# A linear-attention mixer with an MLP on one core: `wv` loaded ahead of x2, x2 and x3 in halves, and the first jobs in another order

## The chip, the core and the metric

The kernel runs on one core of a Trainium2 chip. It has five engines with an instruction stream each: TensorE (PE, matmul; PEld is its weight load), VectorE (DVE), ScalarE (ACT), GpSimd (POOL) and SyncE (SP). DMAs are issued from SP and from ACT. The metric is device time of one execution in microseconds, the median of several. The kernel before was timed three times.

## What is computed

The input x has 2048 tokens of 448 features. It is normalised; two branches work on the result, and both are added to x:

```python
x = A_x
xn = _layernorm(x, axis=-1)
return x + _A_ref(xn, A_wqkv, A_w_phi, A_wo) + _B_ref(xn, B_w1, B_w2, B_w3, B_w4)

# A: 16 heads of 28
qkv = x @ wqkv
pq, pk = q @ w_phi, k @ w_phi                       # per head
phi_q = concat(softmax(pq), softmax(-pq)); phi_k likewise
kv = phi_k^T v;  z = sum over tokens of phi_k
o = (phi_q kv) / (phi_q z + 1e-6);  return o @ wo

# B: four channel groups of gelu(layernorm(x) @ w1) shifted by 1, -1, 2, -2 tokens
h = gelu(layernorm(x) @ w1)
x1 = x + concat(shifted quarters of h) @ w2
return x1 + gelu(layernorm(x1) @ w3) @ w4
```

(The lines under A and B are shortened; the branch B normalises xn once more, which in the kernel is the same normalised tile, with its own epsilon taken in the sums.)

## The kernel before

**Recorder.** The program is written as a sequence of operations with an engine each (`Recorder.op`, L67). `solve` (L76) works out which operation has to wait for which, and every engine plays its own operations strictly in the order in which they were recorded. So the order of the text is the order on each engine, and an operation that waits holds back all that stand behind it on its engine. All matmuls carry line 204, PE transposes 208, ScalarE activations 212, element-wise operations 216, DMAs 219 (transposing) and 222.

**Loads (L351 to L388).** x is loaded as 16 tiles of 128 tokens (x0 to x15, `load_x`); weights with 448 input rows in two halves of 256 rows that overlap by 64 (`load_half`), so that each holds two chunks of 128 rows. The order on SP's queue is x0, x2, second half of `wv`, x4, second half of `w1`, x6 and x7, x8 to x11, x12 to x15, `w_phi`, then transposing DMAs of the q and k weights (`load_wT`, the first of which waits for `wv`); on ACT's queue x1, x3, first half of `wv`, x5, first half of `w1`.

**Layer norm (L453 to L487), tile by tile.** In the lists, `("m", i)` is the statistics of tile i on VectorE (`bn_stats`, `bn_aggr`), `("r", i, n)` the inverse root for n tiles from i on GpSimd (a power of -0.5, `ln_scale`), `("a", i)` subtracting and scaling on VectorE into `xn`, `("p", i)` the same on GpSimd. Tile 1's sums are made on ScalarE instead (`ln1_sums`, L470), and `("v", 1)` is its aggregate on VectorE.

**First jobs (L945 to L969).** TensorE works on the two halves of its rows at once: LO, partitions 0 to 63, and HI, 64 to 127. The jobs that `chain` (L560) plays are
- `XT(i, b)`: eight PE transposes of normalised tile i, four in each half, into PSUM banks b and b+1, then an eviction to `xnT` on ScalarE (`xn_out`, L514); `XD(i)` does the transposition by a DMA instead;
- `ZV(i)`: V of tile i, seven matmuls of 448 columns on `wv` (four in one half, three in the other), then the eviction `EV` to `vaug`;
- `ZW(g, m)`: the first MLP matrix for four tiles, seven matmuls of 512 columns on `w1`, then a GELU (`EW`);
- `FO`: the product of the k or q weights with the feature map; `ZR`, `HF`: the remaining channels of `w1`, and the first q, k and `w2` products;
- `L(...)`: layer-norm steps; `do(f)`: anything else.

For a `zip` job (ZV, ZW, ZR) `chain` puts out the LO matmuls at once and keeps the HI matmuls in a list `upper`; they are put out between later LO matmuls, not before `lag` columns (600) after the last LO matmul of their job, since both write the same PSUM bank. `inside(n, job, inner)` puts an inner job after n LO matmuls.

`spin(n, cols)` (L491) issues n dummy matmuls on all 128 rows into bank 7, on a tile `busy` that a VectorE memset has filled: 39 of 128 columns at the start, and five of 256 after the transposes of tile 0.

**The rest** is one list played in order (L1034 to L1054): feature maps, attention sums, `w2`, the second layer norm, `w3`, `w4`, `wo` and the stores.

Of the kernel before, what the change touches and what calls it, by code (L numbers as in the profile page):

```python
# [6 lines left out]
ACT = mybir.ActivationFunctionType  # L7
# [217 lines left out]
def bass_parallel_sum__linear_kernel_hedgehog__mixer_s_mlp__prompt_kernel(  # L225
# [17 lines left out]
    with es:  # L243
# [107 lines left out]
        def load_x(i, n, eng="SP"):  # L351
            R.dma(xtok[:, i:i + n, :], x2d[128 * i:128 * (i + n), :].rearrange("(j p) d -> p j d", p=128), eng)

        def load_rows(dst, src):
            R.dma(dst[:, 0:3, :], src[0:384, :].rearrange("(c p) d -> p c d", p=128))
            R.dma(dst[0:64, 3, :], src[384:448, :])
# [5 lines left out]
        def load_half(dst, src, h, eng="SP"):  # L362
            R.dma(dst[:, 2 * h:2 * h + 2, :], src[192 * h:192 * h + 256, :].rearrange("(c p) d -> p c d", p=128), eng)
# [5 lines left out]
        load_x(2, 1)  # L369
        load_x(3, 1, "ACT")  # L370
        load_half(wv, wv_d, 1)
        load_half(wv, wv_d, 0, "ACT")
        load_x(4, 1)
        load_x(5, 1, "ACT")
        load_half(w1, B_w1, 1)
        load_half(w1, B_w1, 0, "ACT")
# [13 lines left out]
        def load_w2():  # L390
            R.dma(w2[:, 0:NH, :], B_w2[0:REST, :].rearrange("(m p) d -> p m d", p=128))
            for h in range(2):
                R.dma(w2[64 * h:64 * h + 64, NH, :], B_w2[REST:D, :])

        def load_w4():
            R.dma(w4[:, :, :], B_w4.rearrange("(c p) d -> p c d", p=128))
# [14 lines left out]
        busy = gT[:, 0, 0, 0:256]  # L411
        R.ew(dve, "memset", busy, 1.0)
# [78 lines left out]
        def spin(n, cols):  # L491
            for _ in range(n):
                R.mm(banks[7][:, 0:cols], busy[:, 0:128], busy[:, 0:cols], True, True)
# [20 lines left out]
        def xn_out(i, b, n, eng):  # L514
            for j in range(n):
                d, a = (xnT[:, :, 128 * (i + j):128 * (i + j) + 128].rearrange("p c (h e) -> p c h e", h=2),
                        xn_t(b)[:, :, 256 * j:256 * j + 256].rearrange("p h (c e) -> p c h e", c=KC))
                if eng == "ACT":
                    R.act(d, a, ACT.Copy)
                else:  # L520
                    R.ew(dve, "tensor_copy", d, a)
# [380 lines left out]
        def do(f, *args):  # L902
            return "do", lambda: f(*args), ()

        def L(*ops):
            return do(ln1, *ops)
# [4 lines left out]
        def XT(i, b, n=1, eng="ACT"):  # L911
            return "both", xn_T(i, b, n), ((xn_out, i, b, n, eng),)
# [3 lines left out]

        def ZV(i, *then):
            return "zip", z_v(i, vb[i]), then
# [4 lines left out]
        def inside(n, job, inner):  # L923
            return (*job, (n, inner))
# [15 lines left out]
        def HF(p, n):  # L940
# [4 lines left out]
        vb = {0: 7, 1: 6, 2: 0, 3: 2, 4: 4, 5: 5, 6: 1, 7: 0, 8: 4, 9: 5, 10: 0, 11: 6, 12: 3, 13: 2, 14: 0, 15: 1}  # L945
        gb = ((5, 2, 3), (7, 6, 5), (4, 1, 0), (7, 7, 4))
        spin(39, 128)
        ln1_sums(1)
        chain([
            L(("m", 0), ("m", 2), ("r", 0, 1), ("a", 0), ("m", 3), ("v", 1), ("r", 1, 2), ("a", 2), ("a", 1), ("r", 3, 1)),  # L950
            XT(0, 2, 1, "ACT"), do(spin, 5, 256), L(("a", 3), ("m", 4), ("m", 5), ("r", 4, 1), ("r", 5, 1)),
            inside(1, ZV(0, EV(0, "ACT", 1)), XT(2, 5, 1, "ACT")), XT(3, 3, 1, "ACT"), ZV(2, EV(2, "ACT", 1)),
            inside(1, ZV(3, EV(3, "ACT", 1)), XT(1, 3, 1, "ACT")), ZV(1, EV(1, "ACT", 1)), L(("a", 4), ("m", 7)),
            ZW(0, 0, EW(0, 0, 1)), L(("a", 5)), XT(5, 0, 1, "ACT"),
            L(("m", 6), ("m", 9), ("r", 7, 1), ("m", 8), ("r", 6, 1), ("r", 8, 1), ("a", 7), ("a", 6), ("m", 10)), ZW(0, 2),
            L(("m", 11), ("a", 8)), XD(8), L(("m", 12)), XT(4, 0, 1, "ACT"), L(("r", 9, 1)), ZW(0, 1, EW(0, 1, 2)), L(("a", 9)),
            ZV(4, EV(4, "ACT", 1)), XD(9), XT(7, 0, 1, "ACT"), L(("r", 10, 2), ("a", 10)), XT(6, 6, 1, "ACT"), L(("m", 13)),
            ZV(5, EV(5, "ACT", 1)), do(phi_blocks), ZV(7, EV(7, "DVE", 1)), ZW(1, 1, EW(1, 1, 1)), ZV(6, EV(6, "ACT", 1)),
            L(("p", 11), ("r", 12, 1), ("m", 15)), inside(2, ZW(1, 0, EW(1, 0, 1)), XT(10, 2, 1, "ACT")), L(("r", 13, 1)),
            ZW(1, 2, EW(1, 2, 1)), L(("p", 12), ("r", 15, 1)), inside(3, ZV(8, EV(8, "ACT", 1)), FO(1, 0, 0)), L(("m", 14)),  # L960
            XD(11), L(("r", 14, 1)), do(load_wT, 0, (1, 2, 3)), L(("a", 13)), inside(1, ZV(10, EV(10, "ACT", 1)), FO(1, 0, 1)),
            L(("a", 15)), ZR(0, 7, (rest_out, 0, 7), (rest_T, 0), (h_shift, 0)), ZV(9, EV(9, "DVE", 1)), XT(12, 3, 1, "ACT"),
            L(("p", 14)), do(load_w2), XT(13, 1, 1, "ACT"), ZV(11, EV(11, "ACT", 1)), ZW(2, 2, EW(2, 2, 1)), do(late_3),
            XT(14, 2, 2, "DVE"), ZW(2, 0, EW(2, 0, 1)), ZW(2, 1, EW(2, 1, 1)), do(load_lap, w3, B_w3), FO(1, 2, 0),
            inside(3, ZW(3, 0, EW(3, 0, 1)), FO(1, 2, 1)), ZR(1, 6, (rest_out, 1, 6)),
            inside(3, ZW(3, 2, EW(3, 2, 1)), FO(0, 0, 0)), ZV(15, EV(15, "ACT", 1)), do(kv_ones),
            inside(3, ZW(3, 1, EW(3, 1, 1)), FO(0, 0, 1)), do(rest_T, 1), inside(1, ZV(14, EV(14, "ACT", 1)), FO(0, 2, 0)),
            FO(0, 2, 1), ZV(13, EV(13, "ACT", 1)), ZV(12, EV(12, "DVE", 1)), HF(0, 0), do(kv_picks), HF(1, 0), HF(2, 0), HF(0, 1),
            do(h_shift, 1), HF(1, 1), do(load_w4), HF(2, 1)], 600, 1)  # L969
# [60 lines left out]
        def wo_in():  # L1030
            load_lap(wo, A_wo)
# [3 lines left out]
            (T, 0), (T, 1), (k0, 1), (w0, 2), (kn, 0), (k1, 1), (w1_, 2), (lo, 0), (q0, 1), (k0, 2), (kx, 0), (k1, 2), (kn, 1), (w0, 4),  # L1035
            (kx, 1), (q1, 1), (T, 2), (T, 3), (q0, 2), (lo, 1), (w1_, 4), (kn, 2), (q1, 2), (T, 4), (T, 5), (lo, 3), (k0, 3), (K, 0), (k1, 3), (kn, 3),
            (kx, 2), (lo, 2), (kx, 3), (q0, 3), (sc, 0), (K, 1), (q1, 3), (T, 6), (T, 7), (A, 1), (A, 0), (k0, 4), (G, 0), (A, 3), (w0, 6),
            (A, 2), (K, 2), (k1, 4), (G, 1), (G, 2), (K, 3), (G, 3), (q0, 4), (w1_, 6), (q1, 4), (k0, 5), (K, 4), (kn, 4),
            (w0, 8), (k1, 5), (q0, 5), (kx, 4), (K, 5), (lo, 4), (w1_, 8), (kn, 5), (q1, 5), (K, 6), (k0, 6), (w0, 10),
            (k1, 6), (kx, 5), (q0, 6), (w1_, 10), (lo, 5), (q1, 6), (k0, 7), (K, 7), (kn, 6), (k1, 7), (q0, 7), (lo, 6),  # L1040
            (K, 8), (q1, 7), (lo, 7), (w0, 12), (kn, 7), (wo_in,), (kx, 6), (a, 0), (sc, 4), (w1_, 12), (b, 0), (A, 4),
            (G, 4), (A, 6), (K, 9), (A, 5), (G, 5), (G, 6), (a, 1), (K, 10), (A, 7), (K, 11), (b, 1), (a, 2), (K, 12),
            (b, 2), (kx, 7), (a, 3), (w0, 14), (a, 4), (G, 7), (lo, 9), (b, 3), (K, 13), (b, 4), (K, 14), (K, 15), (a, 5),
            (kc,), (w1_, 14), (b, 5), (kb,), (a, 6), (b, 6), (lo, 8), (N, 0), (T, 8), (a, 7), (lo, 11), (lo, 10), (f, 1, 0), (N, 1), (T, 9),
            (b, 7), (a, 8), (sc, 8), (A, 10), (A, 8), (b, 8), (f, 2, 0), (lo, 12), (A, 9), (G, 8), (A, 11), (G, 9), (a, 9),
            (G, 10), (G, 11), (a, 10), (b, 9), (lo, 13), (N, 2), (T, 10), (f, 3, 0), (b, 10), (a, 11), (f, 4, 0), (lo, 14), (N, 3), (T, 11),
            (b, 11), (a, 12), (f, 1, 1), (S, 0), (lo, 15), (N, 4), (T, 12), (sc, 12), (b, 12), (f, 2, 1), (A, 13), (A, 15), (a, 13),
            (f, 3, 1), (S, 1), (b, 13), (f, 4, 1), (a, 14), (a, 15), (A, 14), (A, 12), (S, 2), (N, 5), (T, 13), (f, 1, 2), (G, 12),
            (G, 13), (b, 14), (f, 2, 2), (b, 15), (S, 3), (N, 6), (T, 14), (a, 16), (f, 3, 2), (b, 16), (a, 17), (f, 4, 2), (a, 18),
            (G, 14), (S, 4), (b, 17), (S, 5), (N, 7), (T, 15), (f, 1, 3), (G, 15), (N, 8), (a, 19), (f, 2, 3), (b, 18), (f, 3, 3),  # L1050
            (b, 19), (f, 4, 3), (a, 20), (N, 9), (a, 21), (b, 20), (f, 1, 4), (a, 22), (N, 10), (b, 21), (S, 6), (f, 2, 4),
            (a, 23), (f, 3, 4), (b, 22), (f, 4, 4), (b, 23), (N, 11), (a, 24), (f, 1, 5), (S, 7), (a, 25), (N, 12),
            (f, 2, 5), (b, 24), (b, 25), (N, 13), (f, 3, 5), (a, 26), (f, 4, 5), (S, 8), (a, 27), (S, 9), (N, 14), (b, 26),
            (b, 27), (S, 10), (f, 1, 6), (f, 2, 6), (S, 11), (N, 15), (f, 3, 6), (S, 12), (S, 13)])  # L1054
# [34 lines left out]
```

## Time and profile before

| | us |
|---|---|
| median of three runs (lowest, highest) | 174.25 (173.88, 174.35) |
| the profiled execution | 174.06 |
| its span, first to last instruction | 172.3 |
| DVE, ACT, POOL busy | 110.9, 82.0, 90.0 |
| first matmul on `wv` | 7.57 |
| first matmul on `w1` | 11.20 |

"Busy" of TensorE counts from the issue of a matmul to its modelled end; matmuls overlap, and two run side by side on the two row halves, so busy time alone doesn't say how much was done. Times in the profile count from the first instruction of the span. The granted TensorE clock is listed as 1.00 for all stretches, but the first 128-column dummies start 107 ns apart (39 in 4.17 us), and the five 256-column ones after 5.65 us 109 ns apart: the clock doubles at about 5.1 us.

The engines during the first 14 us, as stretches: TensorE busy 5.12 of the first 7.57 us, nearly all of it dummies; 2.87 of 3.05 us from 7.57 to 10.62; 3.33 of 3.38 us to 14.00; 16.00 of 16.00 us from there to 30. VectorE is busy for 2.95 of the 3.05 us from 7.57 to 10.62, and 3.27 of the next 3.38.

### The profile page before, as it was taken

The page shows a single profiled execution, that of the slowest core. Times are in us where ns is not written, and L with a number is a line of the kernel's source. Part 1 is how long each engine was busy: PE and PEld are TensorE (multiplying, and loading weights), DVE is VectorE, ACT ScalarE, POOL GpSimd, SP SyncE. Part 2 cuts the span into 40 slices and gives each one's busy share as a digit, 9 for nine tenths or more (in the row PEclk, how much of TensorE's full clock was granted, in tenths as well). Part 3 has the DMA queues.
Part 4 walks back from the last instruction along what each step waited for, and adds up shares of the span by engine and source line. Part 5 has one row for each costly group of instructions (what it writes and reads, how often), then busy time and mean ns, then how long its engine had stood idle before and what let it go on. Part 6 is the DMA issues. An engine that isn't in the chain of part 4 may idle for free.

```text
span 172.3 us, 5315 instructions
## 1 busy us (share of the span) xinstructions
PE 166.9 (97%) x2308; PEld 96.6 (56%) x2308; DVE 110.9 (64%) x251; ACT 82.0 (48%) x107; POOL 90.0 (52%) x121
## 2 busy tenths in 40 slices
PE   7799999999999999999999999999999999999994
PEld 7545888874555555554544554554545545555563
DVE  3799943749999989918955873525817416474621
ACT  4478876777987899646133322133133212044000
POOL 5456970004779999860574289332441522724540
PEclk9999999999999999999999999999999999999999
DMA  5995546499998955161057557554961120233331
GB/s 127 330 248 92 104 67 158 87 352 220 334 159 174 135 124 138 21 76 30 11 114 97 111 105 146 94 103 106 136 135 34 30 57 4 57 34 84 88 87 50
DMA packets 51111, 20.07 MB, mean 116 GB/s; under 512 B 42256, under 2 KB 50384, under 8 KB 51088
## 3 DMA queue, kind: packets, MB, share of 16 engines
q1 hardware_dynamic: 49968, 18.86, 56.0%
q10 hardware_dynamic: 1120, 0.87, 1.6%
q8 instruction: 18, 0.29, 0.8%
q14 instruction: 5, 0.04, 0.1%
HBM read 7.14 MB, written 1.84 MB: 52 GB/s over the span
## 4 chain that ended last, share of the span: by engine, by line
PE 92%; DMA 3%; ACT 1%; DVE 1%; issue 0%; ACTq 0%
PE banks L204 91%; DMA wv<-in_A_wqkv_dram 3%; PE banks L208 1%; ACT xnT L212 1%; DVE wpq L216 1%; ACT vaug L212 0%; ACTq L222 0%; ACT L366 0%; DVE vaug L216 0%
## 5 line engine op out<-in xcount | busy, mean ns | idle before, releaser
L212 ACT ACTIVATE phik<-banks 128x1024 bf16<-128x1024 f32 (+1 forms) x44 | 42.2, 986 | 63.6 <-PE banks L204 63.4
L204 PE MATMUL banks<-gT,w 64*128 64x512 bf16 x392 | 49.2, 376 | 0.1
L216 DVE TENSOR_TENSOR vaug<-banks,vaug 128x464 f32<-128x464 f32 (+3 forms) x65 | 32.8, 513 | 20.6 <-PE banks L204 18.9
L204 PE MATMUL banks<-w,phik 64*128 64x448 bf16 (+3 forms) x434 | 45.2, 343 | 0.0
L216 POOL TENSOR_TENSOR xnT<-vaug 128x196 bf16<-128x196 f32 (+1 forms) x32 | 18.1, 587 | 47.8 <-DVE vaug L216 47.8
L204 PE MATMUL banks<-wv,xnT 64*128 64x448 bf16 (+3 forms) x222 | 32.8, 346 | 1.4 <-DMA wv<-in_A_wqkv_dram 1.2
L204 PEld LDWEIGHTS banks<-w,phik 64*128 64x128 bf16 (+1 forms) x434 | 22.9, 94 | 19.4 <-issue 0.4
L722 POOL TENSOR_TENSOR phik<-phik,rks 128x1792 bf16<-128x1792 bf16 x8 | 25.6, 3214 | 10.7 <-DVE rks L216 10.5
L204 PEld LDWEIGHTS banks<-gT,w 64*128 64x128 bf16 x392 | 18.0, 94 | 18.7 <-PE banks L204 1.1
L204 PEld LDWEIGHTS banks<-wv,xnT 64*128 64x128 bf16 (+1 forms) x222 | 13.8, 94 | 10.0 <-ACT xnT L212 1.6
L216 POOL TENSOR_TENSOR vaug<-xn,xtok 128x448 f32<-128x448 bf16 x16 | 16.2, 1033 | 0.2 <-DVE vaug L216 0.2
L216 DVE TENSOR_REDUCE ksum<-phik 128x64 f32<-128x1792 bf16 x8 | 16.0, 1994 | 0.0
L216 POOL TENSOR_TENSOR rs<-mv,mhalf 128x1 f32<-128x1 f32 (+2 forms) x18 | 12.4, 694 | 6.6 <-DVE mv L216 6.6
L204 PE MATMUL banks<-xnT,w 64*128 64x512 bf16 x84 | 15.7, 377 | 0.0
L216 DVE RECIPROCAL vaug<-banks 128x16 f32<-128x16 f32 x16 | 4.0, 252 | 17.4 <-PE banks L204 17.4
L204 PE MATMUL banks<-wpk,xnT 64*128 64x448 bf16 x112 | 14.9, 350 | 0.1
L212 ACT ACTIVATE hi<-banks 128x896 bf16<-128x896 f32 x16 | 13.8, 931 | 1.0 <-PE banks L204 1.0
L204 PE MATMUL banks<-wpq,xnT 64*128 64x448 bf16 x112 | 14.2, 349 | 0.0
L204 PE MATMUL banks<-w,hT 64*128 64x448 bf16 x96 | 12.9, 349 | 0.0
L216 DVE TENSOR_TENSOR xn<-banks,xn 128x512 bf16<-128x512 f32 (+1 forms) x16 | 9.0, 606 | 3.0 <-PE banks L204 2.9
L216 DVE BATCH_NORM_STATS2 st<-xn 128x6 f32<-128x448 bf16 x16 | 9.4, 589 | 0.0
L216 DVE BATCH_NORM_STATS2 st<-xtok 128x6 f32<-128x448 bf16 x15 | 9.1, 606 | 0.0
(72 smaller groups left out, 165.4 us busy)
## 6 DMA issues: line engine op xcount, KB each, us to landing
w<-in_B_w_dram SPq DMA_DIRECT2D x2, 896.0 KB, 5.7
out_dram<-vaug SPq DMA_DIRECT2D x15, 112.0 KB, 2.0
w<-in_B_w_dram SPq DMA_DIRECT2D x1, 1568.0 KB, 10.0
xtok<-in_A_x_dram SPq DMA_DIRECT2D x2, 448.0 KB, 7.4
wv<-in_A_wo_dram SPq DMA_DIRECT2D x2, 224.0 KB, 2.9
xtok<-in_A_x_dram SPq DMA_DIRECT2D x3, 112.0 KB, 2.6
xtok<-in_A_x_dram ACTq DMA_DIRECT2D x3, 112.0 KB, 2.8
w<-in_B_w_dram SPq DMA_DIRECT2D x1, 336.0 KB, 4.3
```

The source lines that it names most:

```text
L204: self.op("PE", lambda e: e.matmul(out, lhsT, rhs, start=start, stop=stop, skip_group_check=True), [out], [lhsT, rhs], tile=self._tile(lhsT))
L208: self.op("PE", lambda e: e.transpose(out, in_, ident), [out], [in_, ident], tile=self._tile(in_))
L212: self.op("ACT", lambda e: e.activation(out, in_, func, **kw), [out], [in_] + aps)
L216: self.op(eng, lambda e: getattr(e, name)(out, *args, **kw), [out], aps)
L722: R.op(pool, lambda e: e.tensor_tensor(ph, ph, wide, op=ALU.mult), [ph], [ph, wide, *after])
```

## The change

The transfers get another order, and x2 and x3 go in halves of 64 tokens, one on each queue. The halves of `wv` and `w1` swap queues:

```diff
+        def load_xh(i):
+            for h, eng in enumerate(("SP", "ACT")):
+                R.dma(xtok[64 * h:64 * h + 64, i, :], x2d[128 * i + 64 * h:128 * i + 64 * h + 64, :], eng)
...
         load_x(0, 1)
         load_x(1, 1, "ACT")
-        load_x(2, 1)
-        load_x(3, 1, "ACT")
-        load_half(wv, wv_d, 1)
-        load_half(wv, wv_d, 0, "ACT")
+        load_half(wv, wv_d, 0)
+        load_half(wv, wv_d, 1, "ACT")
+        load_xh(2)
+        load_xh(3)
         load_x(4, 1)
         load_x(5, 1, "ACT")
-        load_half(w1, B_w1, 1)
-        load_half(w1, B_w1, 0, "ACT")
+        load_half(w1, B_w1, 0)
+        load_half(w1, B_w1, 1, "ACT")
```

The dummy operand is a constant that the framework sets up, no longer a tile with a memset; `spin` always takes 128 columns, and `hold` makes short dummy groups on both row halves:

```diff
-        busy = gT[:, 0, 0, 0:256]
-        R.ew(dve, "memset", busy, 1.0)
+        busy = nc.const_aps.tensor(1.0, [128, 128], BF16)
+        R.rows[busy.tensor.name] = (2, False)
...
-        def spin(n, cols):
+        def spin(n):
             for _ in range(n):
-                R.mm(banks[7][:, 0:cols], busy[:, 0:128], busy[:, 0:cols], True, True)
+                R.mm(banks[7][:, 0:128], busy, busy, True, True)
+
+        def hold(b, n):
+            return [[(banks[b + k][:, 0:128], busy[r, :], busy[r, :], True) for _ in range(n)]
+                    for k, r in enumerate((slice(0, 64), slice(64, 128)))]
...
+        def HD(b, n):
+            return "both", hold(b, n), ()
```

The first jobs are re-ordered, roots are taken tile by tile, GpSimd applies tiles 3, 7, 8, 10, 12 and 14 (before: 11, 12 and 14), and `lag` goes from 600 to 200. The head of the two lists:

```diff
-        spin(39, 128)
+        spin(30)
         ln1_sums(1)
         chain([
-            L(("m", 0), ("m", 2), ("r", 0, 1), ("a", 0), ("m", 3), ("v", 1), ("r", 1, 2), ("a", 2), ("a", 1), ("r", 3, 1)),
-            XT(0, 2, 1, "ACT"), do(spin, 5, 256), L(("a", 3), ("m", 4), ("m", 5), ("r", 4, 1), ("r", 5, 1)),
-            inside(1, ZV(0, EV(0, "ACT", 1)), XT(2, 5, 1, "ACT")), XT(3, 3, 1, "ACT"), ZV(2, EV(2, "ACT", 1)),
-            inside(1, ZV(3, EV(3, "ACT", 1)), XT(1, 3, 1, "ACT")), ZV(1, EV(1, "ACT", 1)), L(("a", 4), ("m", 7)),
-            ZW(0, 0, EW(0, 0, 1)), L(("a", 5)), XT(5, 0, 1, "ACT"),
+            L(("m", 0), ("r", 0, 1), ("a", 0), ("v", 1), ("m", 2)), HD(3, 3),
+            L(("r", 1, 1), ("m", 3), ("r", 2, 1), ("r", 3, 1)), do(spin, 3), L(("a", 2)), do(spin, 3), XT(0, 2, 1, "ACT"),
+            L(("a", 1), ("m", 4)), HD(6, 3), L(("m", 5)), HD(4, 3), L(("m", 7), ("p", 3)), HD(6, 3), L(("r", 4, 1)),
+            ZV(0, EV(0, "ACT", 1)), L(("a", 4)), XT(2, 1, 1, "ACT"), do(spin, 3), L(("m", 6), ("r", 5, 1)),
+            XT(1, 5, 1, "ACT"), inside(2, ZV(2, EV(2, "ACT", 1)), XT(3, 1, 1, "ACT")), L(("m", 8)), ZV(1, EV(1, "ACT", 1)),
+            L(("r", 7, 1), ("p", 7), ("r", 6, 1), ("r", 8, 1), ("m", 11), ("a", 5), ("p", 8)), ZV(3, EV(3, "ACT", 1)),
+            XT(4, 1, 1, "ACT"), ZW(0, 0, EW(0, 0, 1)), L(("a", 6)), ZV(4, EV(4, "ACT", 1)), L(("m", 9)), XT(7, 0, 1, "ACT"),
...
-            do(h_shift, 1), HF(1, 1), do(load_w4), HF(2, 1)], 600, 1)
+            HF(0, 1), do(h_shift, 1), HF(1, 1), do(load_w4), HF(2, 1)], 200, 1)
```

The loads of `w2`, `w3`, `w4` and `wo` get a parameter for the queue, which stays SP, and `w3` is loaded by two calls in place of one that issues the same two DMAs. The long list of the rest is wrapped differently and holds the same entries in the same order. A few PSUM banks of V and of the first MLP matrix are numbered differently.

## The prediction

> **What bounds the kernel now.** The first view is the page's busy line: TensorE is at work for 97% of the span, no other engine above 64%.
>
> ```profile
> PE 166.9 (97%) x2308; PEld 96.6 (56%) x2308; DVE 110.9 (64%) x251; ACT 82.0 (48%) x107; POOL 90.0 (52%) x121
> ```
>
> The second is the chain of waits in order of time (start, length, what). From 10.62 us on it is TensorE almost without a break; before that it is the landing of `wv`, and then the evictions of transposed tiles.
>
> ```profile
> 1.74 5.70 DMA wv<-in_A_wqkv_dram
> 7.43 0.14 issue
> 7.57 0.21 PE banks L204
> ...
> 9.54 0.54 ACT vaug L212
> 10.08 0.50 ACT xnT L212
> 10.58 0.05 issue
> 10.62 1.56 PE banks L204 x12
> ...
> 86.56 83.30 PE banks L204 x1012
> ```
>
> So everything after about 10.6 us is a queue of matmuls that moves as a block. The change leaves their number and the whole written order after the first jobs as they are; its worth is how much useful TensorE work is done by the time TensorE stops starving. The third view is the DMA issues, asked for the stretches in which they were issued (KB, then us to landing): x2 and x3 (issued at 1.25), `wv` (1.71 and 1.74), x4 and x5 (2.18 and 2.22).
>
> ```profile
> xtok<-in_A_x_dram SPq DMA_DIRECT2D x1, 112.0 KB, 2.6
> xtok<-in_A_x_dram ACTq DMA_DIRECT2D x1, 112.0 KB, 2.8
> wv<-in_A_wqkv_dram SPq DMA_DIRECT2D x1, 224.0 KB, 4.8
> wv<-in_A_wqkv_dram ACTq DMA_DIRECT2D x1, 224.0 KB, 5.7
> xtok<-in_A_x_dram SPq DMA_DIRECT2D x1, 112.0 KB, 5.4
> xtok<-in_A_x_dram ACTq DMA_DIRECT2D x1, 112.0 KB, 5.8
> ```
>
> That is x2 in SBUF at 3.85, x3 at 4.1, `wv` at 6.5 and 7.43, x4 at 7.6, x5 at 8.0. The fourth is busy time by stretch; the last two numbers are DMA share and GB/s. Both queues are never empty here, yet the rate falls around 4 us, where `wv` starts, and is full again by 6.
>
> ```profile
> 2.00:4.00 2.00, 2.00 (x21) 2.00 (x20) 1.06 (x3) 0.57 (x3) 1.26 (x8) 1.00 0.96 248
> 4.00:5.00 1.00, 1.00 (x12) 1.00 (x11) 0.89 (x4) 0.94 (x4) 0.56 (x1) 1.00 0.61 181
> 5.00:6.00 1.00, 1.00 (x18) 0.74 (x17) 0.97 (x4) 0.45 (x3) 0.00 (x0) 1.00 1.03 314
> 6.00:7.00 1.00, 0.37 (x4) 0.09 (x1) 0.20 (x2) 0.36 (x1) 0.71 (x2) 1.00 1.06 351
> ```
>
> The last is the timeline of VectorE and TensorE, from which the durations come.
>
> ```profile
> 5.43 0.29 PE L208 MATMUL banks<-ident,xn 64*128 64x64 bf16 x8
> 7.03 1.06 DVE L216 TENSOR_SCALAR xn<-xtok,mv,rs 128x512 bf16<-128x512 bf16 x3 [0.82 <-POOL rs L216]
> 8.00 0.62 DVE L216 BATCH_NORM_STATS2 st<-xtok 128x6 f32<-128x448 bf16 x1
> 8.77 0.58 DVE L216 BATCH_NORM_STATS2 st<-xtok 128x6 f32<-128x448 bf16 x1
> ```
>
> One tile's statistics hold VectorE for 0.75 us (8.00 to 8.77), an apply for 0.41, and by 7.03 VectorE has the statistics of tiles 0 to 3 behind it.
>
> **Transfers.** What is moved: the two halves of `wv` go from third to second place on both queues, x2 and x3 behind them, each now as 64 tokens on each queue. That is one more issue on each queue ahead of x4 (0.45 us by the rows of 0.39 to 0.49); x4 lands 5.4 us after its issue, so it is waiting in a backlog and the issue is hidden. On ScalarE's queue it moves the sums of tile 1 from 3.51 to about 3.65, hidden too, as will be seen. With 115 kB a tile and 229 kB a half of `wv`, the first two windows bring 22 + 496 kB by 4.0, 699 by 5.0, 1013 by 6.0, 1364 by 7.0. `wv` ends at 917 kB in the order of issue, a place passed at 5.7, and landed 0.8 and 1.7 us later; x4 and x5 end at 1147 kB, passed at 6.4, and landed 1.2 and 1.6 later: the slowest of the 16 engines trails. Now `wv` ends at 688 kB, passed at 4.95: **landing at 5.8 and 6.7**. x2 ends at 803 kB, passed at 5.3, and needs both queues, so the later lag: **6.95**. x3 ends at 917: **7.3**. Bounds for x2: 5.85 with the lag of x1 (229 kB passed near 2.9, landed 3.44), 5.1 if the dip around 4 us vanishes as well (1.25 us at some 150 instead of 370 GB/s is worth 0.74), and 8.0 if it lands where x5 did. I take 6.95, since x4 is the nearest row.
>
> The Trainium skill (DMA: Bandwidth & Descriptors, Rules for kernel authors) speaks against the halves: two transfers to disjoint partition halves serialize, sharing the same 16 engines, so one transfer of 128 partitions should be used. By that rule x2 would come no earlier than x3, at 7.3, and the sum below would be 0.35 higher; the trace of before has no transfer in halves.
>
> **VectorE behind x2.** Its new order is statistics 0, apply 0, aggregate 1, statistics 2, statistics 3, apply 2, apply 1, statistics 4, 5, 7, apply 4. It waits at statistics 2 for x2; queued behind are statistics 3 and, above all, apply 1, whose own root would be there by 6.2. From 6.95: statistics 2 to 7.75; statistics 3 to 8.6 with its aggregate; meanwhile GpSimd takes root 2 (0.56, done 8.5); apply 2 8.6 to 9.0; apply 1 to 9.35. TensorE's next job after V of tile 0 is the transpose of tile 2: 9.05, eviction by ScalarE 0.33 later and 0.60 long (5.43, 5.76 and 6.36 for tile 0): **V of tile 2 from 10.05**. Tile 3 is now applied on GpSimd (0.19 + 0.77 to 0.91, after root 3 at 9.2): 10.3, transposed inside V of tile 2 without loss. Tile 4 is applied at 12.05, just as TensorE arrives. After that tiles 7 and 8 are on GpSimd also, so VectorE has three applies less (1.2 us) against 1.5 us of statistics done later: about even, and I find no further wait for TensorE.
>
> **Useful work.** A pair of 448-column matmuls on the two row halves takes 0.19 us (six in 0.74 us from 10.62, the last pair draining 0.35), so one is worth 0.095; a tile's eight transposes 0.11. Before, by 10.62 the timeline has 17 matmuls on `wv` and four tiles of transposes: 1.6 + 0.45 = 2.05 us, as if TensorE had started at 8.57. After, by 10.05 four matmuls and three tiles of transposes: 0.38 + 0.33 = 0.7, as if at 9.35. That is +0.78. Before then loses 0.2 between 12.83 and 13.04 waiting for an eviction; after loses 0.05 at tile 4. **Sum so far +0.63.**
>
> **Edits that cost little.** The dummy matmuls need no VectorE memset now and start near 0.8 instead of 1.25; 30 + 3 + 3 + 3 of 0.107 again fill up to the first transposes at 5.4. They read a constant, a form that no row shows; were each a quarter longer (1.0 us in all), the transposes of tile 0 would be late by 1.0, which the wait for tile 2 until 9.05 covers. The nine pairs after it run at 0.055 in the eviction of tile 0 (0.6 us, idle but for five 256-column ones before). The three full-array ones after the transposes of tile 2 cost 0.16 and two changes of row mode of some 0.12 (5.53 to 5.65), 0.4 in all; their cover is the wait for the eviction until 10.05, without it they would cost 0.4. Two joint roots become four single ones: 1.1 us more on GpSimd, which idles for more than that. The halves of `w1` swap queues (landing 8.9 and 9.2, needed after 11).
>
> The lead by which a group's upper row half follows the lower falls from 600 to 200 columns: its first matmul comes after one lower matmul, not two, so it waits for a result (0.35 us after issue, about 0.05 for the signal) while the second lower matmul queues behind it, due after 0.37. That is 0 to 0.03 for each of the 16 V groups, 0 to 0.4 in all; I take 0.1. **Total +0.73.** The profiled execution took 174.06 (span 172.3, 1.76 around it), 0.19 below the median of 174.25: **174.8 us.**
>
> **Rivals.** First, faster: x2 arrives by 5.7, because the dip and the trailing engine belong to the place that `wv` had and not to `wv`. For it: x1 trailed by 0.55 only, and x5's queue by more than x4's, so the lag isn't fixed; against it: the rate falls just where `wv` begins, and x4, x5 still trail. Every microsecond of x2 is one microsecond of V of tile 2: break-even at 6.2, 0.3% faster from 5.7, and at 5.1 to 5.85 the sum is -1.1 to -0.4: about 173.3. Second, no change: x2 as forecast, but the loss is regained between 14 and 40 us, where the chain has one more hand-over (VectorE `wpq`, 1.10 at 30.18) and the first jobs are re-ordered; 0.5 back gives 174.3. Against it: TensorE is busy for 16.00 of 16.00 us from 14 to 30. Third, worse: the halves gain nothing and x2 lands with x3 at 7.3 (+0.35, 175.2), or both as late as x5 did, at 8.0 (+1.05, 175.8), or TensorE's clock falls in the new idle stretch from 7.1 to 9.05 (clock 1.00 through the 1.2 us before 7.57); it took 3.9 us of dummies to full speed, so half speed over as much would cost 1.9.
>
> **Chances.** Forecast 0.42, first rival 0.34, second 0.12, third 0.12. A difference of 0.3% (0.52 us) is about what can be told from none. The forecast crosses that line at x2 = 6.75, so I count 0.30 of it as slower and 0.12 as no change: faster 0.34, same 0.24, slower 0.42. The likeliest case alone is 174.3 to 175.2; with the other two the range is 173.0 to 175.6, which leaves out the lowest part of the first rival and the clock.
>
> **What would show it.** The landing of x2 (6.95 or below 5.7), the start of VectorE's third statistics, V of tile 2 near 10.05, idle weight loads between 7.1 and 9.05, and no self-waits of TensorE after 14 us. It is wrong if x2 is in before 6.2, or if TensorE shows new waits after 14 us.

## The result and the profile after

| | before | after |
|---|---|---|
| median of six runs (lowest, highest), us | 174.27 (173.79, 174.57) | 176.07 (174.91, 176.82) |
| ratio, with its 95% interval | 1 | 1.0105 [1.006, 1.0151] |
| the profiled execution, us | 174.06 | 175.48 |
| its span, us | 172.3 | 173.8 |

The change made the kernel 1% slower. The profiled execution lost 1.42 us, the medians differ by 1.80. The ratios, here and below, leave out runs more than 1.5% above the fastest of their kernel. On the page, TensorE has 19 matmuls more than before (2327 against 2308) and is still the busiest engine by far:

```profile
PE 167.6 (96%) x2327; PEld 124.2 (71%) x2327; DVE 109.6 (63%) x246; ACT 82.4 (47%) x108; POOL 93.1 (54%) x129
```

The chain of waits of the changed kernel (start, length, what). Its beginning no longer runs through `wv` but through ScalarE's queue of DMA issues and the sums of tile 1. And there is a DMA in it at 62.86, where the chain of before is matmuls alone from 42.07 to 79.98 (its line stands apart):

```profile
1.75 0.55 ACTq L222
2.31 0.03 issue
2.34 0.87 ACTq L222
3.21 0.04 issue
3.24 0.64 ACTq L222
3.89 0.04 issue
3.92 0.45 ACTq L222
4.37 0.04 issue
4.43 0.05 issue
4.48 0.68 ACT xn L481 x2
5.16 0.02 issue
5.18 0.21 ACT mv L212
5.40 0.02 issue
5.42 0.77 ACT xn L483 x2
6.21 0.04 DVE mv L216
...
62.86 4.21 DMA gT<-g_tok
67.07 0.24 issue
67.31 13.83 PE banks L204 x228
```

```profile
42.07 37.91 PE banks L204 x602
```

The DMA issues between 1.65 and 3.5 us (KB each, median us to landing). `wv` was issued at 1.25 on both queues; the issues for x2 and x3 followed as two of 56 KB on each queue:

```profile
wv<-in_A_wqkv_dram SPq DMA_DIRECT2D x1, 224.0 KB, 3.2
wv<-in_A_wqkv_dram ACTq DMA_DIRECT2D x1, 224.0 KB, 3.7
xtok<-in_A_x_dram SPq DMA_DIRECT2D x2, 56.0 KB, 3.3
xtok<-in_A_x_dram ACTq DMA_DIRECT2D x2, 56.0 KB, 3.5
```

So `wv` is in SBUF at 4.5 and 5.0 instead of 6.5 and 7.43, and x2 and x3 follow, with their second halves at 5.35 and 5.71. The busy time by stretch (the last number is GB/s) has the dip of the rate later than before, at 5 to 7 us:

```profile
2.00:4.00 2.00, 2.00 (x21) 1.93 (x19) 0.91 (x3) 0.09 (x1) 1.26 (x8) 1.00 0.98 315
4.00:5.00 1.00, 1.00 (x14) 0.58 (x12) 0.23 (x2) 0.52 (x2) 0.56 (x1) 1.00 1.08 326
5.00:6.00 1.00, 0.60 (x24) 0.52 (x24) 0.41 (x1) 0.94 (x5) 0.00 (x0) 1.00 1.12 213
6.00:7.00 1.00, 0.58 (x14) 0.31 (x8) 0.75 (x3) 0.67 (x3) 0.51 (x1) 1.00 0.81 227
```

VectorE's timeline shows what the statistics of tile 2 (statistics 2) stood behind: the aggregate of tile 1, which waited 0.79 us for ScalarE (`xn`, L483 is the second pass of the sums). Statistics 2 follow without a wait for any DMA:

```profile
6.21 0.20 DVE L216 BATCH_NORM_AGGREGATE mv<-st 128x2 f32<-128x9 f32 x1 [0.79 <-ACT xn L483]
6.33 0.59 DVE L216 BATCH_NORM_STATS2 st<-xtok 128x6 f32<-128x448 bf16 x1
```

and TensorE's timeline has the transposes of tile 2 at 8.29, V of tile 2 at 9.27:

```profile
6.72 0.93 PE L204 MATMUL banks<-wv,xnT 64*128 64x448 bf16 x4 [0.42 <-ACT xnT L212]
8.29 0.29 PE L208 MATMUL banks<-ident,xn 64*128 64x64 bf16 x8 [0.64 <-DVE xn L216]
...
9.27 0.55 PE L204 MATMUL banks<-wv,xnT 64*128 64x448 bf16 x3 [0.19 <-ACT xnT L212]
```

**Where the time went.** Both kernels do the same 2264 useful matmuls (dummies left out), so one can add up their columns in the order of issue (those of half the rows count half) and ask how much later the changed kernel has issued the sum that the kernel before had issued at a given time. This is worked out from the matmuls of the two traces:

| time in the kernel before, us | 9 | 10 | 11 | 14 | 20 | 40 | 65 | 70 | 90 | 100 | 120 | 165 |
|---|---|---|---|---|---|---|---|---|---|---|---|---|
| after is later by, us | 0.89 | 0.68 | 0.29 | 0.07 | 0.09 | 0.07 | 0.07 | 1.15 | 1.17 | 1.44 | 1.42 | 1.47 |

By 14 us the changed kernel has caught up but for 0.1. Nearly all of the loss is made at two places far behind the code that was changed: 1.1 us at 66 and 0.3 at 92. TensorE's timeline at the first place, after:

```profile
65.48 0.73 PE L204 MATMUL banks<-w,hT 64*128 64x448 bf16 x6
66.05 0.35 PE L204 MATMUL banks<-w,hRT 64*128 64x448 bf16 x2
67.31 1.04 PE L204 MATMUL banks<-gT,w 64*128 64x512 bf16 x8 [0.91 <-DMA gT<-g_tok]
```

and before, where the same matmuls on `gT` follow without a gap:

```profile
65.41 0.73 PE L204 MATMUL banks<-w,hT 64*128 64x448 bf16 x6
65.97 0.35 PE L204 MATMUL banks<-w,hRT 64*128 64x448 bf16 x2
66.16 1.03 PE L204 MATMUL banks<-gT,w 64*128 64x512 bf16 x8
```

The transposing DMA that writes this part of `gT` was issued 0.4 us earlier than before (62.86 against 63.26), but took 4.2 us to land in place of 2.5. In the DMA view from 64 to 66 us (packets, MB, share of 16 engines; the last line is the issue with its time to landing) the changed kernel has one packet of a queue that isn't the kernel's own:

```profile
q1 hardware_dynamic: 678, 0.25, 56.2%
q8 instruction: 1, 0.02, 3.8%
gT<-g_tok SPq DMA_TRANSPOSE x1, 4.2
```

and the kernel before has none in that stretch:

```profile
q1 hardware_dynamic: 579, 0.16, 43.9%
gT<-g_tok SPq DMA_TRANSPOSE x1, 2.5
```

That queue carries 18 packets of 16 KB in both kernels. They come every 4 to 12 us, and in the changed kernel's trace TensorE starts 188 to 309 matmuls and weight loads between one and the next. In the changed kernel they start at 57.2, 64.8 and 72.8 us, before at 58.6, 67.6 and 72.9, and each of these takes 0.9 to 1.5 us. The second place looks the same: the transposing DMA `xnT<-xnT` took 4.1 us there in place of 2.4, with such a packet from 91.0 to 92.2; before, the packet starts at 92.6, when that DMA has landed. The Trainium skill (Runtime: NRT & Kernel Launch, Instruction fetch mechanics) says that an engine's instructions are refilled in blocks of 16 KiB, 256 instructions, through a DMA queue of its own, at a cost that is mostly hidden. The trace agrees with the size and the count: a matmul comes with a weight load, and 2 x 2327 / 256 is 18.2. What it says of the cost holds for the engine that fetches: in the kernel before, TensorE has no wait between 14 and 100 us, with ten such packets in that stretch. The experiments ask whether it holds for a DMA that the fetch (so these packets are called from here on) meets.

### The profile page after: what moved, and what is told of

Read it like the earlier page. It is cut to its first block, busy times and chain, and to the rows that moved or that the text cites. A ratio compares the mean times of both kernels' runs of the same rounds, so it can differ in the third digit from the quotient of the medians.

```text
span 173.8 us, 5360 instructions
## 1 busy us (share of the span) xinstructions
PE 167.6 (96%) x2327; PEld 124.2 (71%) x2327; DVE 109.6 (63%) x246; ACT 82.4 (47%) x108; POOL 93.1 (54%) x129
## 4 chain that ended last, share of the span: by engine, by line
PE 75%; DVE 8%; POOL 5%; ACT 3%; DMA 2%; SPq 2%; ACTq 2%; issue 1%
PE banks L204 74%; POOL phik L736 4%; DVE ksum L216 3%; DMA gT<-g_tok 2%; SPq L219 2%; ACTq L222 2%; DVE xn L216 1%; DVE st L216 1%; PE banks L208 1%; ACT phik L212 1%; DVE rks L216 1%; POOL g_tok L216 1%; POOL rs L216 1%; DVE wpq L216 1%; ACT xn L483 0%
## 5 line engine op out<-in xcount | busy, mean ns | idle before, releaser
L212 ACT ACTIVATE phik<-banks 128x1024 bf16<-128x1024 f32 (+1 forms) x44 | 42.2, 987 | 65.0 <-PE banks L204 64.8
L204 PE MATMUL banks<-gT,w 64*128 64x512 bf16 x392 | 51.6, 376 | 1.0 <-DMA gT<-g_tok 0.9
L204 PE MATMUL banks<-w,phik 64*128 64x448 bf16 (+3 forms) x434 | 46.2, 343 | 0.0
L204 PEld LDWEIGHTS banks<-w,phik 64*128 64x128 bf16 (+1 forms) x434 | 35.9, 94 | 6.6 <-issue 0.4
L204 PEld LDWEIGHTS banks<-gT,w 64*128 64x128 bf16 x392 | 27.4, 94 | 11.1 <-issue 1.3
L204 PE MATMUL banks<-wv,xnT 64*128 64x448 bf16 (+3 forms) x222 | 34.3, 346 | 0.7 <-ACT xnT L212 0.6
L204 PEld LDWEIGHTS banks<-wv,xnT 64*128 64x128 bf16 (+1 forms) x222 | 17.6, 94 | 5.7 <-ACT xnT L212 1.4
L216 POOL TENSOR_TENSOR rs<-mv,mhalf 128x1 f32<-128x1 f32 (+1 forms) x20 | 12.9, 654 | 4.2 <-DVE mv L216 4.2
```

The costliest lines, as they stand in the source:

```text
L204: self.op("PE", lambda e: e.matmul(out, lhsT, rhs, start=start, stop=stop, skip_group_check=True), [out], [lhsT, rhs], tile=self._tile(lhsT))
L212: self.op("ACT", lambda e: e.activation(out, in_, func, **kw), [out], [in_] + aps)
L216: self.op(eng, lambda e: getattr(e, name)(out, *args, **kw), [out], aps)
```

## Experiments

Each kernel was timed beside the kernel before on the same chip (medians of the kernel before: 174.0 to 174.2 us). The first theory is the fetch: 19 more matmuls are 38 more instructions, every later fetch comes 38 instructions earlier, and one now falls on a transposing DMA that TensorE waits for. The rivals are that the loss comes from the transfers, or from the new order.

**Fewer dummies in the changed kernel, of the same length in all.** The constant is taken 512 wide, so that longer dummies can be made.

```diff
-        spin(30)
+        spin(11, 349)
```

> The changed kernel with its 30 first dummy matmuls of 128 columns replaced by 11 of 349 columns: the same 3.2 us of dummies, but 19 matmuls (38 TensorE instructions) fewer, the count of the kernel before. Theory 1 (the loss is made at 66 to 67 us and at 92 us, where a 16 KB instruction fetch of TensorE falls on a transposing DMA that TensorE waits for; 38 more instructions have moved the fetches there): the fetches go back to about 67.6 and 92.6 us, the wait of 0.9 us for the transposed g tile is gone, and the span is 1.0 to 1.4 us shorter than the changed kernel's 173.8, time 174.0 to 174.5. Theory 2 (the loss is made in the first 15 us by the order of transfers and jobs): nothing but the dummies changes, so the wait at 67 us stays and the time stays at 175.3 to 176.8.

175.39 us (173.79 to 176.19), 1.0052 [1.0022, 1.0082]. In the profiled execution (span 172.5) the fetches are back at 59.0 and 67.4, TensorE has no wait for `gT`, and the kernel is 0.2 behind the kernel before from 25 us to the end (at 20 it is 0.3 ahead; then TensorE waits for a transposing DMA of `xnT` that met a fetch at 19.5). The loss at 66 is gone with the 19 matmuls. But the median fell by half of it only: five of the twelve runs took 175.3 to 176.2 and list a mean TensorE clock of 0.99, and two others were as slow at 1.00; the rest took 173.8 to 174.8. So something else is in it.

**More dummies in the kernel before.** The order and the transfers stay; five dummies of 256 columns become 24 of 53.

```diff
-            XT(0, 2, 1, "ACT"), do(spin, 5, 256),
+            XT(0, 2, 1, "ACT"), do(spin, 24, 53),
```

> The kernel before with its five 256-column dummies replaced by 24 of 53 columns in the same idle stretch (5.65 to 7.5 us): 19 matmuls more, the count of the changed kernel, and nothing else. Theory 1: the fetches move to about 64.8 and 91 us, the wait for the transposed g tile appears, and the time rises by 1.0 to 1.4 us to 175.2 to 175.7. Theory 2: the dummies end before TensorE has work (7.5 us), so the time stays at 174.0 to 174.5.

175.77 us, 1.0102 [1.007, 1.0135]. TensorE's timeline shows the hole of the changed kernel in the kernel before:

```profile
66.39 0.35 PE L204 MATMUL banks<-w,hRT 64*128 64x448 bf16 x2
67.49 1.04 PE L204 MATMUL banks<-gT,w 64*128 64x512 bf16 x8 [0.74 <-issue]
```

The profile names no releaser here; the answer for the tile `gT` tells what came late:

```profile
DMA to landing us min/median/max: 2.4/2.5/4.1
```

Its fetch starts at 65.2, and its lag behind the kernel before goes from 0.42 at 65 us to 1.33 at 70. Another 0.6 is lost between 20 and 25, where TensorE waits for a transposing DMA of `xnT` that took 5.1 us and met a fetch at 18.2. So 19 matmuls that do nothing, in time that was idle, cost the kernel before as much as the whole change did.

**The transfers alone, in the kernel before**, in its own order of first jobs:

```diff
-        load_x(2, 1)
-        load_x(3, 1, "ACT")
-        load_half(wv, wv_d, 1)
-        load_half(wv, wv_d, 0, "ACT")
+        load_half(wv, wv_d, 0)
+        load_half(wv, wv_d, 1, "ACT")
+        load_xh(2)
+        load_xh(3)
...
-        load_half(w1, B_w1, 1)
-        load_half(w1, B_w1, 0, "ACT")
+        load_half(w1, B_w1, 0)
+        load_half(w1, B_w1, 1, "ACT")
```

> The kernel before with only the transfers of the changed one (wv ahead of x2, x2 and x3 in halves, halves of wv and w1 on the other queues). Theory 1: TensorE's instructions are the same in number, so there is no wait at 67 us; what the transfers do to the first 15 us is small, 174.0 to 174.8. Theory 2: the transfers are the cause (the issues on ScalarE's queue delay the sums of tile 1 by 1 us), and the time is 175 or more.

176.94 us, 1.0155 [1.0126, 1.0184]. Nothing is lost at 66 us, but 2.3 us by 14 us. In this order statistics 2 stand ahead of the apply of tile 0 on VectorE and wait 1.41 us for x2, until 5.68, so that the transposes of tile 0 start at 6.88 in place of 5.43. This kernel's profile also shows a second mechanism, in the busy time by stretch (busy TensorE first, then the other engines; the third number from the end is TensorE's granted clock):

```profile
5.73:9.14 3.41, 1.49 (x23) 0.87 (x24) 2.52 (x9) 0.72 (x3) 1.23 (x2) 1.00 1.02 317
9.14:12.55 3.41, 3.41 (x38) 1.99 (x32) 3.31 (x11) 1.99 (x4) 1.55 (x3) 0.50 1.32 257
12.55:16.00 3.45, 3.40 (x47) 1.70 (x45) 3.31 (x11) 2.72 (x6) 1.97 (x4) 1.00 0.46 90
```

After a stretch of 3.41 us in which TensorE was busy for 1.49 (its longest idle time was 1.28), the clock is halved for exactly the next 3.41 us, in which TensorE had work throughout. That is 1.7 us of work lost, and 0.5 x 3.41 / 174 = 0.01 off the mean clock: the 0.99 in the lists of runs. Here five of six runs list 0.99 or 0.98. The sixth lists 1.00 and still took 176.59, so the clock is not all that these transfers cost in the old order; what its time went into isn't known. The Trainium skill (TensorE: Matmul & The Clock Gate, What's actually happening) gives a free-running window of 3413 ns that looks at how busy the array was, and halves the clock after an idle one; the length agrees, but the window here was idle by half only.

**The new order alone, with the transfers of before** (the diff above the other way round, in the changed kernel).

> The changed kernel with the transfers of the kernel before, all else as changed. Theory 1: the 38 instructions are still there, the fetch still falls near 64.8 us and the wait for the transposed g tile stays: 175.0 to 176.8. Theory 2, as far as the transfers are the cause: 174.5 or less.

175.96 us (174.25 to 178.09), 1.0101 [1.0066, 1.0137]. In the profiled execution (174.25, its fastest) the first jobs are 0.7 us ahead of the kernel before at 20 us: the sums of tile 1 begin at 3.52, V of tile 2 at 8.70, although `wv` is awaited. At 66 it loses 0.9 again, with a fetch at 64.2. So in this execution the new order is better than the old, and the count of matmuls costs its microsecond with the old transfers too. That the new transfers lose the gain shows in the profiles alone: the ratios with the old and the new transfers, 1.0101 and 1.0105, can't be told apart.

**The idle time filled, with 44 and with 63 dummies.** The short groups become longer (360 columns) and four matmuls of 448 columns follow V of tile 0; the dummies at the start bring the count to that of before, or, as `spin(32, 120)`, to that of the change (`hold` takes the number of columns, and `HL` is `HD` for the lower half alone):

```diff
-            L(("a", 1), ("m", 4)), HD(6, 3), L(("m", 5)), HD(4, 3), L(("m", 7), ("p", 3)), HD(6, 3), L(("r", 4, 1)),
-            ZV(0, EV(0, "ACT", 1)), L(("a", 4)), XT(2, 1, 1, "ACT"),
+            L(("a", 1), ("m", 4)), HD(6, 2, 360), L(("m", 5)), HD(4, 2, 360), L(("m", 7), ("p", 3)), HD(6, 2, 360), L(("r", 4, 1)),
+            ZV(0, EV(0, "ACT", 1)), HL(4, 4, 448), L(("a", 4)), XT(2, 1, 1, "ACT"),
...
-        spin(30)
+        spin(13, 295)
```

> The changed kernel with 44 dummy matmuls as in the kernel before (13 of 295 columns at the start), and with the idle stretches ahead of V of tile 0 and between it and the transposes of tile 2 filled: 12 dummies of 360 columns in place of 18 of 128, and four of 448 on the lower row half. Clock theory (in about half of the executions TensorE is busy for too little of one 3.4 us window between 5 and 10 us and runs the next one at half clock, 1.4 us): all executions at a mean clock of 1.00 and at 173.8 to 174.5, where the same without the fill had 5 of 12 at 0.99 and 175.3 to 176.2. Rival (the scatter is from transfers that come late in some executions): the scatter stays, 173.8 to 176.2, whatever the dummies.

> The same fill, but with 63 dummy matmuls, the changed kernel's own number. Clock theory with instruction fetch: the wait for the transposed g tile near 67 us stays (1 us), the scatter goes: all executions at 175.0 to 175.7, none at 176.6 or more. Rival (late transfers): scatter from 175 to 176.8.

With 44: 174.71 us (174.62 to 175.15, twelve runs, all at clock 1.00), 1.0032 [1.0018, 1.0047]. The spread is gone, 0.5 us against 2.4 without the filling. The filling itself costs: this kernel is 0.5 to 1.0 late over the first 40 us and 0.8 from there on, and its time is above the 173.8 to 174.5 that was expected. With 63: 176.14 us, 1.0106 [1.0083, 1.0128], also all at 1.00, and above the expected 175.0 to 175.7 too. The two differ in the number and the length of the first dummies, which have the same columns in all: 1.43 us for 19 matmuls. The profiled execution of the second was its longest, 177.69; it loses 1.6 us between 65 and 70, and its waits of TensorE from 14 to 100 us are (us in total, times, longest):

```profile
PE banks L204 <- DMA gT<-g_tok: 1.5, 1, 1.5
PE banks L204 <- DMA xnT<-xn: 0.3, 1, 0.3
PE banks L204 <- DMA xnT<-xnT: 0.2, 1, 0.2
```

**x2 and x3 whole, behind `wv`**, with the count of before and the groups of 360 columns, without the four after V of tile 0:

```diff
-        load_xh(2)
-        load_xh(3)
+        load_x(2, 1)
+        load_x(3, 1, "ACT")
...
-        spin(30)
+        spin(17, 226)
```

> The changed kernel with wv still ahead of x2, but x2 and x3 whole, one on each queue (five issues on ScalarE's queue as before, none of 64 rows), 44 dummies, and the dummies ahead of V of tile 0 widened to 360 columns. If the halves cost the first microsecond by their issues (on ScalarE's queue they took 0.55, 0.87 and 0.64 us where a whole tile takes 0.45, and the sums of tile 1 began at 4.48 in place of 3.51): the sums begin at 3.5 to 3.6, VectorE's second statistics of the chain no longer wait for the aggregate of tile 1, V of tile 2 starts near 8.3 in place of 9.27, and the time is 173.5 to 174.3. If wv ahead of x2 is itself the cost, since x2 lands late: statistics 2 wait for x2 until 6 or later, V of tile 2 stays near 9.3, 174.4 or more.

**173.61 us (173.24 to 175.95, twelve runs), 0.9975 [0.9956, 0.9994]**: faster than the kernel before by a quarter of a percent, and faster than the change. ScalarE's timeline shows where the start is better:

```profile
1.74 0.98 ACTq L222 DMA_DIRECT2D xtok<-in_A_x_dram  x2
2.76 0.46 ACTq L222 DMA_DIRECT2D w<-in_B_w_dram  x1
3.55 0.58 ACT L481 ACTIVATE xn<-xtok 128x448 bf16<-128x448 bf16 x1 [1.47 <-DMA xtok<-in_A_x_dram]
```

ScalarE's queue is through with its DMAs at 3.2 in place of 4.37, and the sums begin when x1 is there. Statistics 2 start at 5.43, V of tile 2 at 8.37. This kernel is 0.8 us ahead of the kernel before from 14 us on and 0.7 at the end, and TensorE has no wait at all between 14 and 100 us. One of the twelve runs lists a clock of 0.99.

**The changed kernel with x2 and x3 whole, and nothing else**: the first hunk of the diff above alone, with all 63 dummies.

> The changed kernel with one edit: x2 and x3 are loaded whole, one on each queue, behind wv; all 63 dummies stay, and no idle time is filled. Theory (halves lengthen the first chain of ScalarE and VectorE by about 1 us and so drop the clock; the 19 extra matmuls put an instruction fetch on the transposes of gT): sums of tile 1 near 3.55 us and V of tile 2 near 8.4 as with 44 dummies, useful work ahead of the kernel before by 0.5 to 0.8 us until 65 us, then a loss of 0.9 to 1.4 there, a wait of TensorE for gT; span about 172.5 to 173, time 174.3 to 174.9, and hardly a run with clock 0.99. Rival 1 (the count of matmuls matters only together with a late start, so that with whole tiles it costs nothing): 173.4 to 173.8, no wait at 66 us. Rival 2 (the idle stretch, not the halves, drops the clock): half of the runs at clock 0.99 and 1.4 us longer, median near 175.7.

175.1 us (174.47 to 176.8, eight runs), 1.0077 [1.0039, 1.0116], 0.2 above what the theory said. It is 0.4 ahead at 20 and 65 us, less than the 0.5 to 0.8 of the theory, and 0.8 behind at 70. Its only wait of TensorE from 14 to 100 us:

```profile
PE banks L204 <- DMA gT<-g_tok: 1.0, 1, 1.0
```

That is the theory, and against rival 1: with the better start the fetch (at 64.55) still meets the DMA. Two of eight runs were at 0.99, more than the theory said, though without the filling. x2 was 0.3 late here (statistics 2 waited for it until 5.84), and V of tile 2 began at 8.82.

**Fewer dummies still: 34.** If fetches go by the count, ten matmuls less move them on again:

```diff
-        spin(17, 226)
+        spin(7, 512)
```

> The same with 34 dummies (7 of 512 columns at the start). If the position of the instruction fetches decides what the later waits cost: every fetch comes 20 instructions later, the one near 20 us clears the transposing DMAs of tiles 8, 9 and 11, the one near 67 us stays behind the g tiles, and the profile shows no wait of TensorE for a DMA between 14 and 70 us; 0 to 1.1 us less than with 44. If not: the same time as with 44.

With x2 and x3 whole: 173.9 us, 0.9991 [0.9971, 1.0011]. No wait of TensorE for a DMA from 14 to 100 us with either count, so there is nothing to gain by moving the fetches on. Nor did the fetch near 67 us move: 1316 matmuls are still to come at its start, 1318 with 44. In the profiled execution x2 came at 6.0.

**The transfers of before, with the new order, the groups 448 columns wide, and 44 or 34 dummies.**

> The changed order of jobs with the transfers of the kernel before, 44 dummies, and the dummies ahead of V of tile 0 widened to 448 columns. If the three causes (fetch position, clock, issues on ScalarE's queue) are all: the first 15 us keep the 0.65 us that this order gained with the old transfers, no wait near 67 us, mean clock 1.00: 173.2 to 173.8, faster than the kernel before by 0.2 to 0.5%. If the new order itself costs later: 174.0 or more.

> The changed order with the transfers of the kernel before, as run with 44 dummies (174.41, with waits of 0.5 us each for the transposed tile at 23 us and the transposed rest at 35 us), but with 34. Fetch position: these two waits are gone or moved and the time is 173.4 to 174.0; if they have another cause they stay and the time is 174.2 to 174.6.

174.41 us, 1.0018 [0.9996, 1.004], and 174.28, 1.0004 [0.9987, 1.002]. With 44, TensorE waited for a transposing DMA of `xnT` (issued at 18.4, fetch at 19.8) and for one of `hRT`, and lost 0.6 us at each place. The first took 4.6 us; the second landed in 2.5, so the fetch at 30.6 did not slow it, and why it was late is open. With 34 there is no such wait and 0.3 lost at the second. But `wv` came late in both profiles (first matmul on it at 7.57 and 7.73), and the times can't be told apart: inconclusive. The 173.2 to 173.8 that the three causes together were to give was not reached. By their medians, both are slower than with `wv` first and whole tiles.

**Is it the first MLP matrix that slows `wv` down?** In the kernel before, both halves of `w1` are issued behind x6 and x7:

```diff
-        load_half(w1, B_w1, 1)
-        load_half(w1, B_w1, 0, "ACT")
         load_x(6, 2)
+        load_half(w1, B_w1, 1)
+        load_half(w1, B_w1, 0)
```

> The kernel before with both halves of w1 issued on SP behind x6 and x7, all else as before. If the dip of the DMA rate from 3.5 to 4.75 us belongs to the first reads of wv: it stays there, wv lands at 6.5 and 7.4, and the time stays at 173.8 to 174.5. If it belongs to the issue of w1 (the dip began 0.8 to 1.3 us after that issue in every trace so far): it moves to 4.5 us or later, wv lands by 6, V of tile 0 starts by 6.5 in place of 7.57, and the time is 173.2 to 174.0.

175.0 us, 1.0036 [1.001, 1.0062]. The dip of the rate stayed where it was and `wv` came no earlier (first matmul at 7.51). So it isn't the issue of `w1`. Six of the twelve runs list a clock of 0.99 or 0.98 and took 175.3 to 177.3; those at 1.00 took 174.0 to 174.7.

## Why the prediction was wrong

It said 174.8 us (173.0 to 175.6) and slower as the likeliest by a little. The sign was right by luck: the loss that it forecast, from a late x2, was not there, and another took its place. Both things by which it was to be known as wrong came true: x2 was in before 6.2 (at 5.35), and TensorE has a new wait after 14 us (for `gT`, at 66).

- **"Everything after about 10.6 us is a queue of matmuls that moves as a block."** This is the step that failed. The written order behind the first jobs is unchanged, but where in it an instruction fetch falls, and so which DMA it meets, shifts with the number of TensorE's instructions, and that the change did alter: 63 dummies for 44. The prediction counted the dummies and priced them by their duration, in idle time, at nothing. They cost 1.1 us at 66 and 0.3 at 92 in the profile, 1.43 between two kernels with the same dummy columns. The forecast's +0.73 had no such term.
- **Transfers.** `wv` was forecast for 5.8 and 6.7 and came at 4.5 and 5.0; x2 was forecast for 6.95 and came at 5.35. The lag of the slowest engine did not follow `wv` to its new place, as the first rival held. The dip did not vanish but moved to 5 to 7 us. Its cause is open. The landing also differs between executions: in four other traces with these transfers x2 came at 5.6 to 6.75.
- **"On ScalarE's queue it moves the sums of tile 1 from 3.51 to about 3.65, hidden too."** They began at 4.48. An issue of 64 tokens took 0.55 and 0.87 us in that queue, that of x5 behind them 0.64, where 0.45 each had been taken from the rows of whole tiles. The aggregate of tile 1 stands ahead of statistics 2 on VectorE, so the wait that was forecast for x2 was one for ScalarE, and ended at 6.33 in place of 6.95. The first rival's gain was lost here: with whole tiles statistics 2 start at 5.43 and the kernel is 0.8 ahead.
- **The halves.** The rule of the Trainium skill against halves (DMA: Bandwidth & Descriptors, Rules for kernel authors) was right in its advice: in the three traces with `wv` first and whole tiles the sums of tile 1 began at 3.54 to 3.58, in the five with halves at 4.14 to 4.48 (V of tile 2, which also hangs on x2, at 8.37 to 8.97 with whole tiles, and at 9.27 in the changed kernel and 8.92 with 44 dummies). Its reason, that the data of the two halves serialise, is not what decided here: x2 was in at 5.35, 0.36 ahead of x3; the data came early, the issues came late.
- **V of tile 2 from 10.05, and the sum.** It began at 9.27, 0.78 earlier. The forecast of +0.73 less 0.78 is -0.05, and the table has 0.07 at 14 us: with its start put right, the sum of useful work held.
- **Lag 200 for 600, single roots, constant dummies, short groups.** As forecast: between 14 and 40 us the lag stays at 0.1, and TensorE waits for no root and no dummy.
- **The clock.** "Half speed over as much would cost 1.9" was part of the third rival. Two of the six runs list 0.99 (176.64 and 176.80, 1.2 to 1.3 above the profiled execution), which explains part of why the median is 0.6 above the profile. A third, 176.82, lists 0.999 and stays unexplained.

The profiled execution adds up: 0.1 by 14 us, 1.1 at 66 and 0.3 at 92 make 1.5; the span is 1.45 longer, the time 1.42.

That the 19 matmuls make the DMA late is shown by three pairs of kernels, with and without them. That the fetch does it is read from the traces. In the five kernels with 63 dummies the eighth fetch begins with 1336 to 1348 matmuls still to come, and the DMA of `gT` that TensorE waits for near 66 us takes 4.0 to 4.25 us; in the seven with 44 the fetch begins with 1304 to 1318 to come, in the two with 34 with 1316, and the same DMA takes 2.5. And of the 224 DMAs of `gT` in the fourteen traces, the 151 that overlap no fetch all landed in 2.4 to 2.6 us; all that took more, up to 4.4, met one. How one packet of 1 us holds up such a DMA isn't shown, nor how far a given number of matmuls moves a fetch: ten fewer than 44 did not move this one.

## What to carry to other kernels

A dummy matmul in idle time is free on TensorE and not free in the instruction stream: keep the number of instructions and change their length, and after any change of the count look through the transposing DMAs that TensorE waits for against the packets of its instruction queue. An engine that issues DMAs and computes pays for each issue in its own order; split transfers where no computing stands behind them. Idle time at the start is to be looked at window by window, by the 3.41 us stretches of the granted clock: one that was busy for 1.49 us cost 1.7 us here, although no single idle time in it was longer than 1.28.

## What was not expected of the hardware

- A transposing DMA of `gT` lands in 2.4 to 2.6 us where no 16 KB packet of TensorE's instruction queue overlaps it. Where such a packet begins 0.9 to 2.1 us after the issue (33 times in the fourteen traces), it lands in 3.5 to 4.4, and 1.05 to 1.65 us after the packet has ended: 4.2 after, 4.1 in the kernel before with 19 more matmuls. Before, there was one of 4.2 too, for which TensorE did not wait.
- TensorE's clock was halved for 3.41 us after a stretch of 3.41 with 1.49 us busy, and no idle time over 1.3 us. In the twelve other traces that record it the clock was kept; counted in steps of 3.41 us from the start of the full clock, the least busy such stretch is 5.11 to 8.52 in the kernel before, with 2.21 us. Where between them it turns isn't settled.
- Issuing a DMA of 64 tokens took ScalarE's queue 0.54 to 0.87 us in the five traces with halves (0.55 and 0.87 in the changed kernel), one of 128 tokens in the same place 0.45 to 0.50 in the three with whole tiles.
